# Gate's last and up's first pass, and the scores of two heads, as 64-row pairs on one TensorE array

## The chip, the core and the metric

The kernel runs on one core of a Trainium2 chip. The metric is the device time of one execution in microseconds (us). The core has five engines that run side by side and meet at semaphores: TensorE (PE in the profile, its weight loads PEld), VectorE (DVE), ScalarE (ACT), GpSimd (POOL) and SyncE (SP), which here issues all transfers.

## The reference, cut to what matters

The input is 2048 rows of width 576. Each row is normalised. One branch is causal attention with 32 heads of 18 columns and a window of 256; the other is a bilinear unit of inner width 4608. The output is the input plus their gated product.

```python
qkv = (xn @ wqkv).reshape(B, S, 3, 32, 18)...
scores = einsum("bhqd,bhkd->bhqk", q, k) * 18 ** -0.5      # kept where 0 <= i - j < 256
s = einsum("bhqk,bhkd->bhqd", softmax(scores), v)... @ wo
h = (xn @ w_gate) * (xn @ w_up)
out = x + s * silu(h @ w_down)
```

## The kernel before, in words

**Numbers in two parts.** A float32 operand is kept as two float16 parts, high and low, and a product is made of several float16 passes that add up in one PSUM bank. The normalised input, transposed, lies in `XT`: chunks 0 to 3 are the high parts of features 0 to 511, chunks 5 to 8 their low parts, and chunk 4 has the high parts of the last 64 features in rows 0 to 63 and their low parts in rows 64 to 127. A weight tile `upw` (128 output features) has ten chunks in the same manner: 0 to 4 high, 5 to 9 low; its chunks 4 and 9 hold the last 64 features twice, once in each half of the rows. `w_x_passes` (line 162) lists 14 passes of 128 rows: the 13 of `passes`, and at last chunk 9 of the weights with chunk 4 of `XT`, which adds low weight x high input and low weight x low input of the last 64 features.

**The prologue** (to about 220 us) normalises and transposes, and makes the values (`v_tile`) and queries and keys (`qk_tile`, nine groups `m` by four chunks `c` of 512 rows), which go to DRAM (`qk_d`, `v_d`).

**The main part** is a list of 72 slots: 18 groups `g` of 256 inner features by 4 chunks `c` of 512 rows. A slot has 16 places. The four weight tiles of a slot (gate, up, gate, up) take four places each; in every place the loop at line 716 issues a quarter of the 14 passes and then whatever `todo` has for that place, in the order in which `at(slot, place, f, ...)` put it there. Engines keep this order. Gate's sum is taken out by ScalarE (`gate_out`), up's by VectorE, which multiplies it with gate's (`up_out`). Both use the two PSUM banks named `up` in turn. `down` (line 593) multiplies the result with the down weights, in eight groups of six passes of 288 columns in the slot behind.

**The attention** is spread over slots 1 to 64 and a little beyond: step `s` takes two heads (`j`) and 512 queries, in four blocks `i` of 128 queries by up to 384 keys. `load_k`, `load_q` and `load_v` fetch a slot ahead through SP. `score` (line 486) makes one matmul with 72 contracted rows into one of two PSUM banks `s`, then VectorE masks and takes the largest (`sm`, `mx`, line 495). In the steps of the first chunk there are no earlier keys, so block 0 has 128 columns and block 1 has 256. Queries stand in the 72 rows as high, high, low, low and keys as high, low, high, low. `probs` (ScalarE), `turn_probs` (VectorE or GpSimd for the low part, then a transposing transfer `pt`) and `weigh` (six passes of 37 columns a block on TensorE) follow 2, 4 and 12 places behind the score; `finish` (VectorE and GpSimd) ends the step.

```python
        for n in range(8):
            j, i = divmod(n, 4)
            p = 2 * n
            at(b, p, score, s, j, i)
            at(b, p + 2, probs, s, j, i)
            at(b, p + 4, turn_probs, s, j, i)
            at(b, p + 12, weigh, s, j, i)
```

**The end** (from 1647 us) multiplies the attention with `wo` (`o_out`, line 680) and writes the output. At the very start, `keep_warm` (line 109) issues full passes on zeros, and between them two small float32 matmuls (lines 361 and 366) spread the largest value of the weights over the partitions; the second contracts a single row.

Of the kernel before, what the change touches and what calls it, by code (L numbers as in the profile page):

```python
# [11 lines left out]
F16 = mybir.dt.float16  # L12
# [8 lines left out]
def kernel(  # L21
# [10 lines left out]
    nc = tc.nc  # L32
    x = x[0]
    out = out[0]
    S, D = x.shape
# [29 lines left out]
    const = ctx.enter_context(tc.tile_pool(name="const", bufs=1))  # L65
# [7 lines left out]
    qk_d = [dram.tile([8, 2 * DH, S], F16, name=f"qk_d{i}") for i in range(H // 4)]  # L73
    v_d = dram.tile([S, H * VW], F16, name="v_d")
    o_d = [dram.tile([512, 2 * D], F16, name=f"o_d{i}") for i in range(NCH)]

    XT = const.tile([128, 9, S], F16, name="XT")
    ident = const.tile([128, 128], F32, name="ident")
    ones = const.tile([128, 128], F32, name="ones")

# [5 lines left out]
    def up_ring():  # L86
        return ring.tile([128, 10, 128], F16, name="upw", bufs=8)
# [10 lines left out]
    def bank(name, bufs, shape=(128, 512), dt=F32):  # L98
        return psum.tile(list(shape), dt, name=name, bufs=bufs)
# [43 lines left out]
    def hi(w, rv, s):  # L143
        nc.scalar.activation(w, rv, AF.Copy, scale=s)  # L144

    def lo(w, rv, s, h):
        nc.vector.scalar_tensor_tensor(w, rv, s, h, op0=OP.mult, op1=OP.subtract)  # L147
# [8 lines left out]
    def passes(a, b):  # L156
        r = [(a[:, k], b[:, k]) for k in range(5)]
        r += [(a[:, k], b[:, 5 + k]) for k in range(4)]
        r += [(a[:, 5 + k], b[:, k]) for k in range(4)]
        return r  # L160

    def w_x_passes(w, c):
        b = XT[:, :, c * 512:(c + 1) * 512]
        return passes(w, b) + [(w[:, 9], b[:, 4])]
# [56 lines left out]
    def turn(t):  # L221
        nc.sync.dma_start(XT[:, :, t * 128:(t + 1) * 128], XN.pop(t), transpose=True)

# [11 lines left out]
    def v_tile(t):  # L235
        pv = [bank(("s", "dn", "up", "pv")[t % 4], 2) for _ in range(2)]
        xt = XT[:, :, t * 128:(t + 1) * 128]
        ps = [(b, a) for a, b in passes(wv, xt)] + [(xt[:, 4], wv[:, 9])]
# [19 lines left out]
    UW, DW, RAW, HT, GT, SC = {}, {}, {}, {}, {}, {}  # L258

    def qk_split(m):  # L260
        if m < QM:
            w = UW["q", m] = up_ring()
            r = rqk[:, :, m * 128:(m + 1) * 128]
            hi(w[:, 0:5], r, ps_qk[:, 2:3])
            lo(w[:, 5:10], r, ps_qk[:, 2:3], w[:, 0:5])
# [3 lines left out]
    def qk_tile(w, m, c):  # L269
        ps = bank("up", 2)  # L270
        pl = w_x_passes(w, c)
        for i, (a, b) in enumerate(pl):
            nc.tensor.matmul(ps, a, b, start=i == 0, stop=i == len(pl) - 1)  # L273
        if c == 0:
            QP[m] = qpool.tile([128, 2, S], F16, name="qp", bufs=2)
        q = QP[m][:, :, c * 512:(c + 1) * 512]
        nc.scalar.activation(q[:, 0], ps, AF.Copy, scale=PROJ)  # L277
        nc.vector.scalar_tensor_tensor(q[:, 1], ps, PROJ, q[:, 0], op0=OP.mult, op1=OP.subtract)  # L278
# [20 lines left out]
    def ffn_amax(g, kind, half):  # L299
        if (g, "am") not in SC:  # L300
            SC[g, "am"] = ring.tile([128, 2, 3], F32, name="am", bufs=2)
        r = RAW[g, kind]
        r = r[:, half] if kind == 2 else r[:, :, half * 128:(half + 1) * 128]
        nc.vector.tensor_reduce(SC[g, "am"][:, half, kind:kind + 1], r, axis=AX.X if kind == 2 else AX.XY,  # L304
                                op=OP.max, apply_absolute_value=True)

    def ffn_spread_out(g):
        am = SC.pop((g, "am"))
        nc.vector.tensor_tensor(am[:, 0], am[:, 0], am[:, 1], op=OP.max)
        spread_out(f"f{g}", am[:, 0], 3)  # L310

    def ffn_spread_in(g):
        SC[g, "sp"] = spread_in(f"f{g}", ring, 3)
# [112 lines left out]
    for m in range(QM):  # L426
        for c in range(NCH):
            qk_tile(UW["q", m], m, c)
            if c == 1:
                qk_split(m + 2)  # L430
            if m == 1 and c < 3:
                ffn_amax(0, c, 0)
                ffn_amax(0, c, 1)
            if m == 2 and c == 0:
                ffn_spread_out(0)
            if m == 3 and c == 0:
                ffn_spread_in(0)
                ffn_scale(0)
            if m >= QM - 2 and c >= 2:
                k = 2 * (m - QM + 2) + c - 2  # L440
                up_hi(0, k)
                up_lo(0, k)
        qk_store(m)
        del UW["q", m]
# [3 lines left out]
    att = att_stack.enter_context(tc.tile_pool(name="att", bufs=1))  # L448
# [3 lines left out]
                            fill=-3e38, base=0, channel_multiplier=-1)  # L452
    nc.gpsimd.affine_select(bias[:, 256:384], bias[:, 256:384], pattern=[[-1, 128]], compare_op=OP.is_ge,
                            fill=-3e38, base=0, channel_multiplier=1)
    QS, KS, VT, SM, PP, PT, PVB, OB = {}, {}, {}, {}, {}, {}, {}, {}


    def load_k(s):
        c, u = s // 16, 2 * (s % 16) + H
        k0 = max(0, c * 512 - 256)  # L460
        n = (c + 1) * 512 - k0
        KS[s] = att.tile([128, 2, 768], F16, name="ks", bufs=2)
        d = KS[s][:, :, 768 - n:]
        for a in (0, 36):
            nc.sync.dma_start(d[a:a + 36],
                              qk_d[u // 8][u % 8:u % 8 + 2, :, k0:k0 + n].rearrange("j r n -> r j n"))

    def load_q(s):
        c, u = s // 16, 2 * (s % 16)
        d = QS[s] = att.tile([128, 2, 512], F16, name="qs", bufs=2)  # L470
        for a, r0, r1 in ((0, 0, 18), (18, 0, 36), (54, 18, 36)):
            nc.sync.dma_start(d[a:a + r1 - r0],
                              qk_d[u // 8][u % 8:u % 8 + 2, r0:r1, c * 512:(c + 1) * 512].rearrange("j r n -> r j n"))

    def load_v(s):
        c, p = s // 16, s % 16
# [6 lines left out]
    def first_kb(s):  # L483
        return 2 if s < 16 else 0

    def score(s, j, i):
        lo_ = max(first_kb(s), i) * 128
        hi_ = (i + 3) * 128
        n = hi_ - lo_
        ps = bank("s", 2)  # L490
        nc.tensor.matmul(ps[:, :n], QS[s][0:72, j, i * 128:(i + 1) * 128], KS[s][0:72, j, lo_:hi_],  # L491
                         start=True, stop=True)
        sm = att.tile([128, 384], F32, name="sm_", bufs=4)
        mx = att.tile([128, 2], F32, name="mx", bufs=3)
        nc.vector.tensor_tensor_reduce(sm[:, 384 - n:], ps[:, :n], bias[:, 384 - n:], 1.0, -3e38,  # L495
                                       op0=OP.add, op1=OP.max, accum_out=mx[:, 0:1])
        nc.gpsimd.tensor_scalar(mx[:, 1:2], mx[:, 0:1], sig[:, 1:2], shift, op0=OP.mult, op1=OP.add)  # L497
        SM[s, j, i] = (sm[:, 384 - n:], mx, n)
# [13 lines left out]
        nc.sync.dma_start(pt[:, 0:2 * n // 128], pp[:, 0:2 * n], transpose=True)  # L512

    def weigh(s, j, i):
        if j == 0 and i == 0:
            PVB[s] = bank("pv", 2, (128, 2, 4, 64))
        pt = PT.pop((s, j, i))
        lo_ = max(first_kb(s), i)
        nb = i + 3 - lo_
        for n in range(2 * nb):  # L520
            nc.tensor.matmul(PVB[s][:, j, i, :VW], pt[:, n], VT[s][:, lo_ + n % nb, j * VW:(j + 1) * VW],  # L521
                             start=n == 0, stop=n == 2 * nb - 1)
# [32 lines left out]
    def at(slot, place, f, *a):  # L555
        todo.setdefault(slot * 16 + place, []).append((f, a))

    first_slot = 1
    for s in range(NSTEP):
        b = first_slot + s  # L560
        at(b - 1, 1, load_k, s)
        at(b - 1, 3, load_q, s)
        at(b - 1, 13, load_v, s)
        for n in range(8):
            j, i = divmod(n, 4)
            p = 2 * n
            at(b, p, score, s, j, i)
            at(b, p + 2, probs, s, j, i)
            at(b, p + 4, turn_probs, s, j, i)
            at(b, p + 12, weigh, s, j, i)  # L570
        at(b, 31, finish, s)

    def gate_out(sl, ft, ps):
        g = f_ring("gt")
# [35 lines left out]
    for g in range(NG):  # L610
        b = 4 * g - 4
# [104 lines left out]
    for sl in range(NSLOT + 1):  # L716
        g, c = divmod(sl, NCH)
        for place in range(16):
            if sl < NSLOT:
                k, quarter = divmod(place, 4)  # L720
                if quarter == 0:
                    ps = bank("up", 2)
                    pl = w_x_passes(UW[g, k], c)
                n0 = (14 * quarter + 3) // 4
                n1 = (14 * (quarter + 1) + 3) // 4
                for i in range(n0, min(n1, 14)):
                    a, b = pl[i]
                    nc.tensor.matmul(ps, a, b, start=i == 0, stop=i == 13)  # L728
                if quarter == 3:
                    (gate_out if k % 2 == 0 else up_out)(sl, k // 2, ps)  # L730
                    if c == NCH - 1:
                        del UW[g, k]
            for f, a in todo.pop(sl * 16 + place, []):
                f(*a)
# [33 lines left out]
```

## Time and profile before

| what | before |
|---|---|
| time, median of 3 runs | 1719.51 us (1718.47 to 1720.28) |
| profiled execution: its own time | 1717.89 us |
| profiled execution: span from first to last instruction | 1716.0 us |
| granted TensorE clock, mean | 0.993 |
| TensorE matmuls | 12299 |
| VectorE, ScalarE, GpSimd busy | 73%, 53%, 24% |
| DMA, mean rate | 124 GB/s |

A page of the profile gives one execution: busy time of each engine, the span in slices, the chain of work that ended last, and the costliest groups of instructions. Matmuls are pipelined: one lasts longer than the distance to the next, so their busy times overlap and a price is read from the distance of starts. In the windows, a line has the stretch, then the sum of busy time, then the busy time and count for PE, PEld, DVE, ACT and POOL, the granted clock, the share of the DMA engines and GB/s. In the timeline, a line has start, duration, engine, line, operation, operands and count, and in brackets the idle time before it with what ended it.

### The profile page before, as it was taken

The page shows a single profiled execution, that of the slowest core. Times are in us where ns is not written, and L with a number is a line of the kernel's source. Part 1 is how long each engine was busy: PE and PEld are TensorE (multiplying, and loading weights), DVE is VectorE, ACT ScalarE, POOL GpSimd, SP SyncE. Part 2 cuts the span into 40 slices and gives each one's busy share as a digit, 9 for nine tenths or more (in the row PEclk, how much of TensorE's full clock was granted, in tenths as well). Part 3 has the DMA queues.
Part 4 walks back from the last instruction along what each step waited for, and adds up shares of the span by engine and source line. Part 5 has one row for each costly group of instructions (what it writes and reads, how often), then busy time and mean ns, then how long its engine had stood idle before and what let it go on. Part 6 is the DMA issues. An engine that isn't in the chain of part 4 may idle for free.

```text
span 1716.0 us, 34567 instructions
## 1 busy us (share of the span) xinstructions
PE 1682.3 (98%) x12299; PEld 993.8 (58%) x12299; DVE 1250.8 (73%) x3150; ACT 908.6 (53%) x1562; POOL 403.7 (24%) x870
## 2 busy tenths in 40 slices
PE   6999999999999999999999999999999999999999
PEld 3744445555555555555555555555555555555567
DVE  6442367777878888888878888888888878765544
ACT  4422346555565656565656565666666665632230
POOL 2200013322232323232323232322223222320000
PEclk8999999999999999999999999999999999999999
DMA  7942345464546665757586766657676767541228
GB/s 187 225 121 80 102 110 116 91 128 83 125 83 134 134 146 103 154 112 146 104 171 122 127 141 114 140 111 149 135 147 103 145 107 145 108 104 57 58 59 218
DMA packets 543109, 212.17 MB, mean 124 GB/s; under 512 B 479704, under 2 KB 523992, under 8 KB 542936
## 3 DMA queue, kind: packets, MB, share of 16 engines
q1 hardware_dynamic: 542936, 209.96, 58.2%
q8 instruction: 96, 1.57, 0.4%
q14 instruction: 77, 0.63, 0.1%
HBM read 82.30 MB, written 23.75 MB: 62 GB/s over the span
## 4 chain that ended last, share of the span: by engine, by line
PE 93%; DMA 3%; DVE 2%; SPq 1%; ACT 1%; issue 0%; POOL 0%; ACTq 0%; DVEq 0%
PE up L728 50%; PE dn L603 24%; PE up L273 6%; PE s L491 5%; PE pv L521 4%; PE dn L691 2%; PE up L691 1%; DMA sd_qk<-am_qk 1%; SPq L287 1%; DMA XT<-xh 0%; DMA raw<-in_B_w_gate_dram 0%; DMA xr<-in_A_x_dram 0%; PE s L241 0%; DMA spread<-sd_qk 0%; ACT xn L217 0%
## 5 line engine op out<-in xcount | busy, mean ns | idle before, releaser
L728 PE MATMUL up<-XT,upw 128*128 128x512 f16 x4032 | 1048.5, 379 | 2.4 <-DVE ht L580 2.4
L728 PEld LDWEIGHTS <-upw 128*128 128x128 f16 x4032 | 390.8, 97 | 283.8 <-issue 4.5
L603 PE MATMUL dn<-dnw,hh 128*128 128x288 f16 x3432 | 513.3, 286 | 0.8 <-DVE acc L608 0.8
L603 PEld LDWEIGHTS <-hh 128*128 128x128 f16 x3456 | 336.9, 97 | 192.8 <-issue 0.9
L608 DVE SCALAR_TENSOR_TENSOR acc<-dn,sc,acc 128x288 f32<-128x288 f32 x540 | 277.3, 514 | 165.1 <-PE dn L603 163.3
L497 POOL TENSOR_SCALAR mx<-mx,sig 128x1 f32<-128x1 f32 x512 | 179.7, 351 | 852.9 <-DVE mx L495 819.7
L521 PEld LDWEIGHTS <-pt 128*128 128x128 f16 x2880 | 147.5, 96 | 121.2 <-DMA pt<-pp 0.6
L491 PE MATMUL s<-ks,qs 72*128 72x384 f16 (+2 forms) x512 | 160.3, 313 | 1.3 <-DMA qs<-qk_d 1.3
L521 PE MATMUL pv<-vt,pt 128*128 128x37 f16 x2880 | 152.9, 179 | 0.2 <-DMA pt<-pp 0.2
L575 ACT ACTIVATE gt<-up 128x512 f32<-128x512 f32 x144 | 85.5, 594 | 102.5 <-PE up L728 102.4
L585 ACT ACTIVATE hh<-ht 128x512 f16<-128x512 f32 x144 | 89.7, 623 | 70.3 <-DVE ht L580 70.3
L273 PE MATMUL up<-XT,upw 128*128 128x512 f16 x504 | 110.8, 383 | 7.6 <-ACT upw L144 4.0
L580 DVE SCALAR_TENSOR_TENSOR ht<-up,gt 128x512 f32<-128x512 f32 x144 | 98.8, 686 | 12.9 <-PE up L728 12.4
L590 DVE SCALAR_TENSOR_TENSOR hh<-hh,ht 128x512 f16<-128x512 f16 x144 | 98.0, 681 | 0.0
L304 DVE TENSOR_REDUCE am<-raw 128x1 f32<-128x640 f32 (+1 forms) x108 | 85.3, 792 | 7.8 <-DMA raw<-in_B_w_gate_dram 5.4
L273 PEld LDWEIGHTS <-upw 128*128 128x128 f16 x504 | 49.7, 99 | 68.4 <-issue 7.2
L278 DVE SCALAR_TENSOR_TENSOR qp<-up,qp 128x512 f16<-128x512 f32 x36 | 24.9, 691 | 68.3 <-ACT qp L277 57.6
L277 ACT ACTIVATE qp<-up 128x512 f16<-128x512 f32 x36 | 21.5, 597 | 85.7 <-PE up L273 85.7
L147 DVE SCALAR_TENSOR_TENSOR upw<-raw,sc,upw 128x640 f16<-128x640 f32 x72 | 63.3, 880 | 0.1
L241 PEld LDWEIGHTS <-XT 128*128 128x128 f16 x448 | 45.1, 102 | 26.5 <-issue 8.3
L144 ACT ACTIVATE upw<-raw,sc 128x640 f16<-128x640 f32 x72 | 59.1, 824 | 0.0
L541 POOL CAST ob<-o 128x144 f16<-128x144 f32 x64 | 27.8, 435 | 102.4 <-DVE o L537 102.4
(2195 smaller groups left out, 1890.2 us busy)
## 6 DMA issues: line engine op xcount, KB each, us to landing
raw<-in_B_w_down_dram SPq DMA_DIRECT2D x18, 576.0 KB
ks<-qk_d SPq DMA_DIRECT2D x96, 108.0 KB
raw<-in_B_w_gate_dram SPq DMA_DIRECT2D x18, 512.0 KB
raw<-in_B_w_up_dram SPq DMA_DIRECT2D x18, 512.0 KB
pt<-pp SPq DMA_TRANSPOSE x512
qk_d<-qp SPq DMA_DIRECT2D x56, 144.0 KB
vt<-v_d SPq DMA_DIRECT2D x48, 111.0 KB
v_d<-vo SPq DMA_DIRECT2D x16, 296.0 KB
```

The source lines that it names most:

```text
L273: nc.tensor.matmul(ps, a, b, start=i == 0, stop=i == len(pl) - 1)
L304: nc.vector.tensor_reduce(SC[g, "am"][:, half, kind:kind + 1], r, axis=AX.X if kind == 2 else AX.XY, op=OP.max, apply_absolute_value=True)
L491: nc.tensor.matmul(ps[:, :n], QS[s][0:72, j, i * 128:(i + 1) * 128], KS[s][0:72, j, lo_:hi_], start=True, stop=True)
L497: nc.gpsimd.tensor_scalar(mx[:, 1:2], mx[:, 0:1], sig[:, 1:2], shift, op0=OP.mult, op1=OP.add)
L521: nc.tensor.matmul(PVB[s][:, j, i, :VW], pt[:, n], VT[s][:, lo_ + n % nb, j * VW:(j + 1) * VW], start=n == 0, stop=n == 2 * nb - 1)
L575: nc.scalar.activation(g, ps, AF.Copy, scale=G_SC)
L580: nc.vector.scalar_tensor_tensor(h, ps, U_SC, GT.pop((sl, ft)), op0=OP.mult, op1=OP.mult)
L585: nc.scalar.activation(hh[:, 0], h, AF.Copy, scale=1.0 / LO)
L590: nc.vector.scalar_tensor_tensor(hh[:, 1], hh[:, 0], -LO, h, op0=OP.mult, op1=OP.add)
L603: nc.tensor.matmul(ps[:, :HALF], a, b, start=q == 0, stop=q == len(l) - 1)
L608: nc.vector.scalar_tensor_tensor(d, ps[:, :HALF], SC[g][:, 9:10], d, op0=OP.mult, op1=OP.add)
L728: nc.tensor.matmul(ps, a, b, start=i == 0, stop=i == 13)
```

## The change

**Gate and up.** The 13 passes of `passes` stay as they are. The last pass of gate is cut to rows 0 to 63: chunk 9 of its weights by the high parts of the last 64 features. Up's own such pass becomes its first, on rows 64 to 127, with a copy of those high parts that lies in the new tile `XT2`. Both are issued one behind the other at the end of gate's four places, and the products of low by low parts are left out. The two banks of a gate and up pair are taken together at gate's start.

**Scores.** A head now has 54 rows: queries high, high, low by keys high, low, high. Head 0 of the step stands in rows 0 to 53, head 1 in rows 64 to 117. `score_pair` issues both heads' matmuls of a block at places 3, 7, 11 and 15; the VectorE work of head 0 follows there and that of head 1 two places later. The blocks go in the order block, head instead of head, block. Loads of keys and queries are eight a step instead of five. `load_v` and `finish` go one place back.

In the built program the matmuls and weight loads of the pairs address 64 x 128 parts of the array at rows 0 and 64, 400 of each; all other float16 matmuls address 128 x 128, as all did before.

```diff
+    XT2 = const.tile([128, S], F16, name="XT2")
...
+    def full_passes(w, c):
+        return passes(w, XT[:, :, c * 512:(c + 1) * 512])
+
+    def half_pass(w, c, upper):
+        r = slice(64, 128) if upper else slice(0, 64)
+        return w[r, 9], (XT2[r] if upper else XT[r, 4])[:, c * 512:(c + 1) * 512]
...
+            if m == 0:
+                nc.sync.dma_start(XT2[64:128, c * 512:(c + 1) * 512], XT[0:64, 4, c * 512:(c + 1) * 512])
...
     def load_k(s):
...
-        for a in (0, 36):
-            nc.sync.dma_start(d[a:a + 36],
-                              qk_d[u // 8][u % 8:u % 8 + 2, :, k0:k0 + n].rearrange("j r n -> r j n"))
+        for j in range(2):
+            for a, r1 in ((0, 36), (36, 18)):
+                nc.sync.dma_start(KS[s][64 * j + a:64 * j + a + r1, 768 - n:], qk_d[u // 8][u % 8 + j, 0:r1, k0:k0 + n])
 
     def load_q(s):
...
-        for a, r0, r1 in ((0, 0, 18), (18, 0, 36), (54, 18, 36)):
+        for j in range(2):
+            for a, r1 in ((0, 18), (18, 36)):
...
-        nc.tensor.matmul(ps[:, :n], QS[s][0:72, j, i * 128:(i + 1) * 128], KS[s][0:72, j, lo_:hi_],
-                         start=True, stop=True)
+    def score_pair(s, i):
+        lo_ = max(first_kb(s), i) * 128
+        hi_ = (i + 3) * 128
+        for j in range(2):
+            r = slice(64 * j, 64 * j + 54)
+            ps = SP[s, j, i] = bank("s", 2)
+            nc.tensor.matmul(ps[:, :hi_ - lo_], QS[s][r, i * 128:(i + 1) * 128], KS[s][r, lo_:hi_],
+                             start=True, stop=True)
...
-        at(b - 1, 13, load_v, s)
+        at(b - 1, 14, load_v, s)
         for n in range(8):
-            j, i = divmod(n, 4)
-            p = 2 * n
+            i, j = divmod(n, 2)
+            p = 2 * n + 3
+            if j == 0:
+                at(b, p, score_pair, s, i)
             at(b, p, score, s, j, i)
...
-        at(b, 31, finish, s)
+        at(b, 32, finish, s)
...
-                if quarter == 0:
-                    ps = bank("up", 2)
-                    pl = w_x_passes(UW[g, k], c)
-                n0 = (14 * quarter + 3) // 4
-                n1 = (14 * (quarter + 1) + 3) // 4
-                for i in range(n0, min(n1, 14)):
+                up, w = k % 2, UW[g, k]
+                if place % 8 == 0:
+                    banks = bank("up", 2), bank("up", 2)
+                pl = full_passes(w, c)
+                for i in range((13 * quarter + 3) // 4, (13 * (quarter + 1) + 3) // 4):
                     a, b = pl[i]
-                    nc.tensor.matmul(ps, a, b, start=i == 0, stop=i == 13)
+                    nc.tensor.matmul(banks[up], a, b, start=i == 0 and not up, stop=i == 12 and up == 1)
+                if quarter == 3 and not up:
+                    nc.tensor.matmul(banks[0], *half_pass(w, c, False), start=False, stop=True)
+                    nc.tensor.matmul(banks[1], *half_pass(UW[g, k + 1], c, True), start=True, stop=False)
                 if quarter == 3:
-                    (gate_out if k % 2 == 0 else up_out)(sl, k // 2, ps)
+                    (up_out if up else gate_out)(sl, k // 2, banks[up])
```

More of the change, by code (lines that the diff above doesn't have):

```diff
@@ L454 @@
                             fill=-3e38, base=0, channel_multiplier=1)
-    QS, KS, VT, SM, PP, PT, PVB, OB = {}, {}, {}, {}, {}, {}, {}, {}
+    QS, KS, VT, SP, SM, PP, PT, PVB, OB = {}, {}, {}, {}, {}, {}, {}, {}, {}
     def load_k(s):
@@ L461, in load_k @@
         n = (c + 1) * 512 - k0
-        KS[s] = att.tile([128, 2, 768], F16, name="ks", bufs=2)
-        d = KS[s][:, :, 768 - n:]
-        for a in (0, 36):
-            nc.sync.dma_start(d[a:a + 36],
-                              qk_d[u // 8][u % 8:u % 8 + 2, :, k0:k0 + n].rearrange("j r n -> r j n"))
+        KS[s] = att.tile([128, 768], F16, name="ks", bufs=2)
+        for j in range(2):
+            for a, r1 in ((0, 36), (36, 18)):
+                nc.sync.dma_start(KS[s][64 * j + a:64 * j + a + r1, 768 - n:], qk_d[u // 8][u % 8 + j, 0:r1, k0:k0 + n])
     def load_q(s):
         c, u = s // 16, 2 * (s % 16)
-        d = QS[s] = att.tile([128, 2, 512], F16, name="qs", bufs=2)
-        for a, r0, r1 in ((0, 0, 18), (18, 0, 36), (54, 18, 36)):
-            nc.sync.dma_start(d[a:a + r1 - r0],
-                              qk_d[u // 8][u % 8:u % 8 + 2, r0:r1, c * 512:(c + 1) * 512].rearrange("j r n -> r j n"))
+        QS[s] = att.tile([128, 512], F16, name="qs", bufs=2)
+        for j in range(2):
+            for a, r1 in ((0, 18), (18, 36)):
+                nc.sync.dma_start(QS[s][64 * j + a:64 * j + a + r1],
+                                  qk_d[u // 8][u % 8 + j, 0:r1, c * 512:(c + 1) * 512])
     def load_v(s):
@@ L484, in first_kb, with score @@
         return 2 if s < 16 else 0
-    def score(s, j, i):
+    def score_pair(s, i):
         lo_ = max(first_kb(s), i) * 128
         hi_ = (i + 3) * 128
-        n = hi_ - lo_
-        ps = bank("s", 2)
-        nc.tensor.matmul(ps[:, :n], QS[s][0:72, j, i * 128:(i + 1) * 128], KS[s][0:72, j, lo_:hi_],
-                         start=True, stop=True)
+        for j in range(2):
[3 more added lines that the diff above has]
+                             start=True, stop=True)
+    def score(s, j, i):
+        ps = SP.pop((s, j, i))
+        n = (i + 3 - max(first_kb(s), i)) * 128
         sm = att.tile([128, 384], F32, name="sm_", bufs=4)
@@ L514, in weigh @@
     def weigh(s, j, i):
-        if j == 0 and i == 0:
+        if (j, i) == (0, 0):
             PVB[s] = bank("pv", 2, (128, 2, 4, 64))
```

## The prediction

> **What bounds the kernel now.** I read the page's header and chain first.
>
> ```profile
> span 1716.0 us, 34567 instructions
> PE 1682.3 (98%) x12299; PEld 993.8 (58%) x12299; DVE 1250.8 (73%) x3150; ACT 908.6 (53%) x1562; POOL 403.7 (24%) x870
> ...
> PE 93%; DMA 3%; DVE 2%; SPq 1%; ACT 1%; issue 0%; POOL 0%; ACTq 0%; DVEq 0%
> ```
>
> The reader is to see that TensorE is busy for 98% and carries 93% of the chain that ended last. The windows of the main part ask whether it ever waits there.
>
> ```profile
> 300.00:600.00 300.00, 300.00 (x2253) 177.34 (x2251) 234.58 (x646) 177.54 (x324) 89.21 (x194) 1.00 0.54 111
> ...
> 1200.00:1520.00 320.00, 320.00 (x2500) 189.58 (x2499) 262.79 (x670) 199.96 (x336) 91.80 (x198) 1.00 0.68 130
> 1520.00:1647.00 127.00, 127.00 (x768) 72.29 (x766) 66.28 (x130) 26.12 (x42) 4.07 (x12) 1.00 0.21 48
> ```
>
> It doesn't: the busy time (the second number) equals the stretch. VectorE (the fourth) is at 78 to 82% until 1520 us. So time taken from or put on TensorE in the slots counts in full, until another engine is late. Busy times overlap, so a matmul's price is the distance to the next start.
>
> ```profile
> 1535.97 1.51 PE up L728 x7
> ...
> 799.46 0.10 PEld L491 LDWEIGHTS <-qs 72*128 72x128 f16 x1
> 799.48 0.32 PE L491 MATMUL s<-ks,qs 72*128 72x384 f16 x1
> 799.49 0.26 PEld L728 LDWEIGHTS <-upw 128*128 128x128 f16 x2
> 799.64 0.38 PE L728 MATMUL up<-XT,upw 128*128 128x512 f16 x1
> ```
>
> Seven 512-column passes stand for 1.51 us in the chain, 0.216 us each. A 384-column score is followed after 0.16 us, though it lasts 0.32. And the next weight load starts 0.01 us after a matmul has started: it lies under that matmul and costs nothing.
>
> **What is removed.** *Passes.* 18 weight groups x 4 chunks x 2 gate and up pairs make 144 pairs. Each gives up two full passes and gets two 64-row passes of 512 columns. If those run side by side, one pass is saved: 144 x 0.216 = 31.1 us.
>
> *Scores.* There are 512.
>
> ```profile
> L491 PE MATMUL s<-ks,qs x512: 216/322/497, 218.8 to 1519.9; 72*128 72x384 f16 x150, 72*128 72x128 f16 x11, 72*128 72x256 f16 x10
> ...
> L491 PE MATMUL s<-ks,qs 72*128 72x384 f16 (+2 forms) x512 | 160.3, 313 | 1.3 <-DMA qs<-qk_d 1.3
> ```
>
> By the code 32 have 128 columns, 32 have 256 and 448 have 384. At 0.16 us, and the short ones in proportion (0.05 and 0.11), they take 71.7 + 3.5 + 1.7 = 77 us. Pairing would save half: 38.5. Together 31.1 + 38.5 = 69.6 us over 144 + 256 = 400 pairs, 0.174 us a pair. Going from 72 to 54 rows by itself saves nothing: a pass lasts by its columns.
>
> **What is added on TensorE.** Each pair stands between full-array groups (behind a gate pass and before `weigh`, or behind `weigh` and before `down` or passes), so there are 800 changes between the full array and its halves. No trace row shows this change in float16. The nearest are the two small float32 matmuls at the start: line 366 contracts one row, between full-array warming passes of line 112.
>
> ```profile
> 12.04 0.28 DVE L363 TENSOR_REDUCE mrow<-up 1x1 f32<-1x128 f32 x1 [0.55 <-PE up L361]
> 12.22 0.63 PE L112 MATMUL pv<-idle 128*128 128x512 bf16 x1
> 12.78 0.28 PEld L366 LDWEIGHTS up<-mrow,ones 1*128 1x128 f32 x1 [0.84 <-DVE mrow L363]
> 13.02 0.35 PE L366 MATMUL up<-mrow,ones 1*128 1x1 f32 x1
> 13.30 0.10 PEld L112 LDWEIGHTS <-idle 128*128 128x128 bf16 x1
> ...
> 13.70 1.06 PE L112 MATMUL pv<-idle 128*128 128x512 bf16 x2
> ...
> 13.30:15.00 1.70, 1.70 (x5) 0.58 (x5) 1.46 (x6) 0.83 (x2) 0.00 (x0) 0.50 0.93 347
> ```
>
> *Going in.* The page puts L366's wait down to VectorE, but that had ended at 12.04 + 0.28 = 12.32. The load came at 12.78. Two full passes take 1.06 us and one 0.63, so one streams for 0.43; that of 12.22 streamed until 12.65. So a load for a part of the array did not slip under the matmul ahead: it came 0.13 us after its columns had gone in. *Coming out.* The second one-column matmul starts at 13.02, the full-array load at 13.30: 0.28 later instead of 0.01. Part of this may be the slow float32 load of the matmul itself (0.35 to 0.5 us for two), so it is an upper bound. The granted clock was 0.50 there (column after POOL's), against 1.00 in the slots; a pass streams in 0.43 there and 0.216 here. Taking the array's emptying to go with its clock, as the streaming does, I halve both: 0.065 in, 0.14 out. The bounds: nothing at all below, 0.13 + 0.28 unhalved above.
>
> The Trainium skill, "TensorEngine Tiling (Array Packing)", section Key Properties, says that a change of tiling mode drains TensorE. It gives no price; going in, the late load at 12.78 agrees with it.
>
> *The load that nothing hides.*
>
> ```profile
> 39.62 0.41 PE L241 MATMUL pv<-wv,XT 128*128 128x288 f16 x2
> ...
> 39.90 0.24 PEld L241 LDWEIGHTS <-XT 128*128 128x128 f16 x3 [0.19 <-DMA XT<-xh]
> 39.91 0.42 PE L241 MATMUL s<-wv,XT 128*128 128x288 f16 x2
> ```
>
> After a wait for a transfer the load stands open: the matmul starts 0.01 behind it and the first pair of passes takes 0.42 rather than 0.41. So an open load costs about 0.02 us. A pair has three: going in, the second half's behind the first's, and coming out: 0.06.
>
> *Sum.* A pair costs 0.065 + 0.14 + 0.06 = 0.265 us more than its columns, x 400 = 106 us. Less the 69.6 saved: 36 us slower. On the profiled execution's own time of 1717.9 (its span is 1716.0) this is 1754; the median of the runs shown is 1.6 higher, so I say 1755.5.
>
> **What is moved or added elsewhere costs nothing.** *VectorE and the score banks.* Both banks are now filled at place 4i + 3, but the second is read two places later and wanted back two places after that.
>
> ```profile
> 1009.93 0.32 PE L491 MATMUL s<-ks,qs 72*128 72x384 f16 x1
> ...
> 1011.79 0.54 DVE L495 CUSTOM_DVE_ANT_0 sm__13875<-s,bias 128x384 f32<-128x384 f32 x1
> ...
> 1012.50 0.32 PE L491 MATMUL s<-ks,qs 72*128 72x384 f16 x1
> ```
>
> This is one of the latest reads, behind the work of `finish` and a split of down weights: it ends at 1012.33, 2.4 us after its place, and two places are 2.57. So a cover of 0.17 us is left in such a step and more in others. Were VectorE later, both score matmuls would wait and TensorE's whole queue with them: each 0.3 us too late once a step is 64 x 0.3 = 19 us, which I take at nothing, since slower slots give VectorE more room. *Up's bank* is opened one pass earlier, when `up_out` has had most of four places to empty it. *SP.* A step issues eight loads of queries and keys instead of five.
>
> ```profile
> 806.86 0.90 SPq L465 DMA_DIRECT2D ks<-qk_d  x2
> ...
> 809.77 1.06 SPq L472 DMA_DIRECT2D qs<-qk_d  x3
> ...
> SPq L512 <- DVE pp L510: 282.9, 162, 3.1
> ```
>
> At 0.35 to 0.45 us each, three more are 1.3 us in a step of 16 places, 20.5 us. Behind them stand the transposes of the probabilities, which wait for VectorE's `pp` for 283 us in total, so the queue has room, and `weigh` comes eight places (10 us) after its transpose was asked for. The loads are a slot early, and 108 rows of each instead of 144 move. If the cover failed, 64 steps x 1.3 = 83 us would be the limit. The four copies into `XT2` are issued during the first projection, long before slot 0. `score`, `load_v` and `finish` move by up to three places with all that follows them, which only shifts the attention by 4 us inside slots that end 127 us before the last.
>
> **Rivals.** *1, faster: no drain.* The row-tiled load may slip ahead like any other, float32 having been the reason at 12.78. Then a pair costs at most its three open loads, 0.06 x 400 = 24 us, and the change gives 46: 1674. With these hidden too it gives 69.6: 1650. It decides for this side as soon as both changes of a pair together take less than 0.174 − 0.06 = 0.114 us. For it: TensorE's loads are early everywhere else, and the exit row is clouded by the float32 load. Against: VectorE's end at 12.32 explains nothing of the entry at 12.78. The Trainium skill, "TensorE: Matmul & The Clock Gate", Part 3, has row tiles start about 4 ns apart, with a measured 3.07 times for four; no run here shows it, and by it alone this rival's 1650 would hold.
>
> *2, much slower: the halves take turns.* If the second half streams after the first, nothing is saved and the 106 us stay: 1717.9 + 106 = 1824. For it: no two matmuls in this trace run side by side. Against: they share neither rows nor banks. The same time comes from a drain that does not go with the clock: 0.13 + 0.28 + 0.06 = 0.47, x 400 = 188, less 69.6: 1836.
>
> *3, no difference:* both ways cost 0.065, with 0.06 of loads 0.19 a pair: 76 − 69.6 = 6 slower, 1724; a little less and it is even.
>
> **How the numbers follow.** Forecast (a drain each way that goes with the clock, 1724 to 1790, the upper end with half of the unhalved excess): 0.60. Rival 1: 0.24. Rival 2 with the unhalved drain: 0.12. Rival 3, even: 0.04. About 0.2% is what a measurement of this kernel can tell from no change. So faster 0.24, same 0.04, slower 0.72. A range from 1674 to 1824 leaves out the lower half of rival 1 and a part of rival 2, together under 2 in 10; the forecast's own is 1724 to 1790.
>
> **What the profile after would show.** Right: the load of each half pair starts after the columns of the matmul ahead are through, not 0.01 us after its start, and the load of the full group behind it likewise; the two halves start within 0.03 us of each other; the windows stay full, as these gaps lie inside the modelled ends of matmuls, and a slot between 300 and 1500 us takes about 0.5 us more than before. Wrong: loads that stay early around pairs (rival 1), a second half that starts 0.2 us after the first (rival 2), TensorE waiting for VectorE's reads of the scores, or for keys and queries.

## The result, and the profile after

The changed kernel takes 1733.64 us (median of 4 runs, 1733.52 to 1733.91) against 1719.55 for the kernel before: 14.1 us slower, a ratio of 1.0083 with a 95% interval of 1.0065 to 1.0100. The forecast was 36 us slower; the direction was right, the size 2.5 times too large. The measured time lies in the lower part of the stated range of 1724 to 1790.

The page's header and chain of the changed kernel:

```profile
span 1732.1 us, 34687 instructions
...
PE 1695.7 (98%) x12299; PEld 961.2 (55%) x12299; DVE 1229.2 (71%) x3150; ACT 901.8 (52%) x1562; POOL 417.5 (24%) x870
...
PE 93%; DMA 3%; DVE 2%; SPq 1%; ACT 1%; issue 0%; POOL 0%; ACTq 0%; DVEq 0%
```

Still 98% busy and 93% of the chain: what changed is the length of TensorE's own work. In the windows of the main part the busy time still fills the stretch, though the gaps below are in it: they are hidden by the modelled ends of matmuls, and only distances of starts show them.

```profile
300.00:600.00 300.00, 300.00 (x2219) 168.88 (x2218) 226.93 (x640) 171.90 (x318) 89.77 (x192) 1.00 0.51 107
```

The counts tell more: 2219 matmuls stand in this stretch, 2253 stood in it before. A part of this is that the changed kernel comes to 300 us some 5 us earlier in its list of work, so slots are compared below.

One pair of gate and up in the timeline of the changed kernel (start, duration; L747 are full passes, L750 and L751 the halves, L539 the weighing passes behind):

```profile
559.91 0.38 PE L747 MATMUL up<-XT,upw 128*128 128x512 f16 x1
560.22 0.09 PEld L750 LDWEIGHTS <-upw 64*128 64x128 f16 x1 [0.42 <-issue]
560.23 0.09 PEld L751 LDWEIGHTS <-upw 64*128 64x128 f16 x1
560.23 0.39 PE L750 MATMUL up<-XT,upw 64*128 64x512 f16 x1
560.23 0.39 PE L751 MATMUL up<-XT,upw 64*128 64x512 f16 x1
...
560.54 0.10 PEld L539 LDWEIGHTS <-pt 128*128 128x128 f16 x1 [0.23 <-issue]
560.55 0.19 PE L539 MATMUL pv<-vt,pt 128*128 128x37 f16 x1
```

The full pass of 559.91 has streamed by 560.12 (0.213 us for 512 columns: the full pass behind a score pair starts 0.266 after its second half with 384 columns and 0.159 with 128, so 256 columns take 0.107); the load for the first half comes 0.1 later, at 560.22. Both halves start together. They have streamed at 560.44; the full-array load behind them comes at 560.54, 0.1 later again. Two loads that were under the matmul ahead now stand open. A score pair looks the same (L505, with the down passes L623 behind):

```profile
1009.65 0.34 PE L505 MATMUL s<-ks,qs 54*128 54x384 f16 x2
1009.92 0.30 PE L623 MATMUL dn<-dnw,hh 128*128 128x288 f16 x1
...
1030.30 0.34 PE L505 MATMUL s<-ks,qs 54*128 54x384 f16 x2
```

Two 384-column scores in 0.27 us, where each alone took 0.16: side by side, yet 0.1 behind. The same block one slot later starts at 1030.30: a slot with attention takes 20.65 us, against 20.50 before. In the slots without attention only the gate and up pairs are left. Here are the first full passes of two neighbouring slots there, of the changed kernel and then of the kernel before:

```profile
1610.06 0.38 PE L747 MATMUL up<-XT,upw 128*128 128x512 f16 x1
...
1628.02 0.38 PE L747 MATMUL up<-XT,upw 128*128 128x512 f16 x1
```

```profile
1594.19 0.38 PE L728 MATMUL up<-XT,upw 128*128 128x512 f16 x1
...
1612.16 0.38 PE L728 MATMUL up<-XT,upw 128*128 128x512 f16 x1
```

17.96 and 17.97: there the change does nothing. So the loss sits in the scores. From the starts of each slot: 0.307 us in each of the 15 slots after slot 1 that have the scores of the first chunk (these are shorter, so that pairing saves less), 0.146 in most others with attention, together some 11.4. Nearly all the rest of the 16.1 between the two profiled spans is the prologue (slot 0 starts 3.7 later, 1.6 of it before the change touches anything) and one wait at slot 1.

### The profile page after: what moved, and what is told of

The parts are those of the page before. It is cut to its first block, busy times and chain, and to the rows that moved or that the text cites. A ratio compares the mean times of both kernels' runs of the same rounds, so it can differ in the third digit from the quotient of the medians.

```text
span 1732.1 us, 34687 instructions
## 1 busy us (share of the span) xinstructions
PE 1695.7 (98%) x12299; PEld 961.2 (55%) x12299; DVE 1229.2 (71%) x3150; ACT 901.8 (52%) x1562; POOL 417.5 (24%) x870
## 4 chain that ended last, share of the span: by engine, by line
PE 93%; DMA 3%; DVE 2%; SPq 1%; ACT 1%; issue 0%; POOL 0%; ACTq 0%; DVEq 0%
PE up L747 46%; PE dn L623 26%; PE up L283 6%; PE pv L539 5%; PE s L505 4%; PE up L750 3%; PE dn L711 2%; PE up L711 1%; SPq L297 1%; DMA sd_qk<-am_qk 1%; DMA XT<-xh 0%; DMA xr<-in_A_x_dram 0%; PE s L251 0%; DMA spread<-sd_qk 0%; DMA raw<-in_B_w_gate_dram 0%
## 5 line engine op out<-in xcount | busy, mean ns | idle before, releaser
L747 PE MATMUL up<-XT,upw 128*128 128x512 f16 x3744 | 902.3, 379 | 0.0
L747 PEld LDWEIGHTS <-upw 128*128 128x128 f16 x3744 | 366.4, 98 | 337.5 <-issue 2.4
L623 PE MATMUL dn<-dnw,hh 128*128 128x288 f16 x3432 | 515.7, 286 | 0.8 <-DVE acc L628 0.8
L515 POOL TENSOR_SCALAR mx<-mx,sig 128x1 f32<-128x1 f32 x512 | 163.8, 320 | 843.6 <-DVE mx L513 755.5
L623 PEld LDWEIGHTS <-hh 128*128 128x128 f16 x3456 | 295.8, 97 | 113.1 <-issue 42.6
L539 PEld LDWEIGHTS <-pt 128*128 128x128 f16 x2880 | 137.1, 96 | 119.6 <-issue 28.3
L539 PE MATMUL pv<-vt,pt 128*128 128x37 f16 x2880 | 154.2, 180 | 0.0
L283 PE MATMUL up<-XT,upw 128*128 128x512 f16 x504 | 112.5, 387 | 8.6 <-ACT upw L146 4.6
L283 PEld LDWEIGHTS <-upw 128*128 128x128 f16 x504 | 50.1, 99 | 70.7 <-issue 9.9
L505 PE MATMUL s<-ks,qs 54*128 54x384 f16 (+2 forms) x512 | 83.6, 323 | 0.1
L751 PE MATMUL up<-XT,upw 64*128 64x512 f16 x144 | 55.6, 386 | 4.5 <-DVE ht L600 4.5
```

Source lines behind the costliest of these rows:

```text
L505: nc.tensor.matmul(ps[:, :hi_ - lo_], QS[s][r, i * 128:(i + 1) * 128], KS[s][r, lo_:hi_], start=True, stop=True)
L623: nc.tensor.matmul(ps[:, :HALF], a, b, start=q == 0, stop=q == len(l) - 1)
L747: nc.tensor.matmul(banks[up], a, b, start=i == 0 and not up, stop=i == 12 and up == 1)
```

## The experiments

The kernel before was run again beside the experiments, with a median of 1720.45 us beside the first four and of 1721.67 beside the last two; each ratio is to the kernel before that ran beside it, and differences to the changed kernel are differences of medians.

**Theory A**, formed from that trace: a change from the whole array to its halves and back costs a fixed price, whatever the pair does; the halves do run side by side. Medians of the distances of starts over all pairs: 0.312 from a full 512-column pass to the half pass, instead of 0.216 (in: 0.096); 0.003 between halves; 0.318 to 0.319 from the second half to the next full matmul (out: 0.105 over the 0.213 that stream); and the first full matmul after it is followed 0.012 later than its like. That is 0.216 a pair for gate and up, within 0.001 the pass saved; 0.206 for scores (0.110 to 0.111 instead of 0.025 behind a 37-column pass), more than the 0.162 or less that they save. **Theory B**: these changes of mode, between the whole array and its halves, are cheap, and the loss comes from the new order, the later reads by VectorE and the additional loads.

**Pairs of gate and up only**, scores as before:

```diff
-                    nc.tensor.matmul(ps, a, b, start=i == 0, stop=i == 13)
+                    nc.tensor.matmul(banks[up], a, b, start=i == 0 and not up, stop=i == 12 and up == 1)
+                if quarter == 3 and not up:
+                    nc.tensor.matmul(banks[0], *half_pass(w, c, False), start=False, stop=True)
+                    nc.tensor.matmul(banks[1], *half_pass(UW[g, k + 1], c, True), start=True, stop=False)
```

> Only the gate and up half passes run in pairs; scores as before (72 rows, whole array). Theory A (each change between the whole array and its halves costs a fixed price, read in the trace after as 0.096 in and 0.117 out for such a pair, 0.003 between the halves; nothing else matters): a pair pays 0.216 and saves 0.216, so 1719 to 1721 us, no difference from before, and a slot without attention takes 17.96 us as before. Theory B (the changes cost little, the loss comes from the new order of the scores, their later reads by VectorE and the eight loads): the pairs' gain shows here, up to 31 us, 1689. The recorded forecast's price of 0.265 a pair would give 1727.

Measured: 1721.06 us against 1720.45, a ratio of 1.0009 (0.9999 to 1.0018). As theory A has it: 31 us of passes are saved and paid back.

**Scores over all rows**, the changed kernel's order, loads and places kept:

```diff
-            nc.tensor.matmul(ps[:, :hi_ - lo_], QS[s][r, i * 128:(i + 1) * 128], KS[s][r, lo_:hi_],
+            nc.tensor.matmul(ps[:, :hi_ - lo_], QS[s][:, j, i * 128:(i + 1) * 128], KS[s][:, lo_:hi_],
```

> The changed kernel with its order, loads and places, but each head's score contracts all 128 rows of the array (queries padded with zero rows in a tile of their own, keys of both heads as loaded), so the scores change no mode. Theory A: a score pair costs 0.086 + 0.003 + 0.117 = 0.206 and saves 0.162 (384 columns), 0.108 (256) or 0.055 (128); without it a slot gets 0.155 us shorter, and 0.32 in the first sixteen: 48 x 0.155 + 16 x 0.32 = 12.5 us, 1721. Theory B: order and loads stay, so 1733.

Measured: 1720.10, a ratio to the kernel before of 0.9999 (0.9990 to 1.0009), so 13.5 less than the changed kernel. Order, loads and later reads cost nothing that the time shows: theory B falls. (From the second chunk of rows on, a slot even takes 20.47 us, 0.03 less than before.) This is also the answer on the cover that the prediction named for them.

**Score pair straight behind the half pair** at places 3 and 11:

```diff
+            if j == 0 and i % 2 == 0:
+                beside[b * 16 + p] = s, i
...
                     nc.tensor.matmul(banks[1], *half_pass(UW[g, k + 1], c, True), start=True, stop=False)
+                    if sl * 16 + place in beside:
+                        score_pair(*beside.pop(sl * 16 + place))
```

> The changed kernel, but at places 3 and 11 the score pair is issued straight behind the gate and up half pair, ahead of the weighing passes, so both share one way in and one way out. Theory A: 128 x (0.086 + 0.117) = 26 us less than the changed kernel, 1708, faster than before by 12. Theory B: 1733, as only 0.15 us of order changes. If the price is for every matmul on a half rather than for the change of mode: 1733 too.

Measured: 1710.06, ratio 0.9943 (0.9926 to 0.9959): 23.6 less than the changed kernel, and faster than before. One of these places in its timeline (L753 and L754 are the halves, L505 the scores):

```profile
554.33 0.38 PE L750 MATMUL up<-XT,upw 128*128 128x512 f16 x1
554.64 0.09 PEld L753 LDWEIGHTS <-upw 64*128 64x128 f16 x1 [0.42 <-issue]
...
554.65 0.39 PE L753 MATMUL up<-XT,upw 64*128 64x512 f16 x1
554.65 0.39 PE L754 MATMUL up<-XT,upw 64*128 64x512 f16 x1
554.66 0.10 PEld L505 LDWEIGHTS <-qs 54*128 54x128 f16 x2
554.87 0.33 PE L505 MATMUL s<-ks,qs 54*128 54x384 f16 x2
555.13 0.22 PEld L539 LDWEIGHTS <-pt 128*128 128x128 f16 x6 [0.37 <-issue]
```

Within the mode the score loads are early again, 0.01 us after the halves start, and the scores follow the halves at 0.22, one pass's length. One way in, one way out, for four matmuls. So the price belongs to the change of mode, not to a matmul on a half. A slot of the later chunks takes 20.24 us here against 20.65 in the changed kernel, and the 0.41 is two ways in and out, as theory A has it. The 2.3 or so that are missing from the 26 are lost once, at slot 1, which takes 25.8 us against 23.5: there TensorE waits 5.7 us for VectorE instead of 4.5, and the granted clock behind that wait is 0.54 from 230 to 234 us, where it is 0.78 in the changed kernel.

**The same, and the lone blocks over all rows** (places 7 and 15):

```diff
-            r = slice(64 * j, 64 * j + 54)
+            r = slice(64 * j, 64 * j + 54) if i % 2 == 0 else slice(0, 128)
```

> As the adjacent version, and the other two blocks of a step (places 7 and 15) have their scores over all 128 rows of the array, with zero-padded queries, so that no pair stands alone. Theory A: 112 lone pairs of 384 columns lose 0.044 each and 16 of 256 lose 0.1: 6 to 7 us less than the adjacent version, 1701 to 1702. Theory B: no less than the adjacent version.

Measured: 1703.39, ratio 0.9898 (0.9883 to 0.9913): 6.7 less again. This version is 17 us faster than the kernel before and 30 faster than the changed one.

**Halves apart**: gate and up pairs only, but each half alone at the end of its own four places.

```diff
+                if quarter == 3:
+                    nc.tensor.matmul(banks[up], *half_pass(w, c, up == 1), start=False, stop=True)
```

> As the version with gate and up pairs only, but each half pass is issued alone at the end of its own four places, so that nothing runs beside it and each pays its own way in and out. Theory A: a pair costs 0.096 + 0.213 + 0.003 + 0.117 - now two single halves at 0.096 + 0.213 + 0.117 = 0.43 each: 144 x 0.43 = 61 us more than the pairs-only version (1721), 1782. If two halves streamed one after the other even as a pair (the recorded rival 2): 144 x 0.21 = 31 us more, 1752. If only a pair pays, not a single half: no more than 31, too.

Measured: 1779.42 us, ratio 1.0342 (1.0299 to 1.0385): 58.4 more than with pairs, against 61 expected and 31 if the halves of a pair took turns. A single half pays what a pair pays:

```profile
465.12 0.09 PEld L739 LDWEIGHTS <-upw 64*128 64x128 f16 x1 [0.42 <-issue]
465.13 0.39 PE L739 MATMUL up<-XT,upw 64*128 64x512 f16 x1
465.44 0.24 PEld L613 LDWEIGHTS <-hh 128*128 128x128 f16 x3 [0.23 <-issue]
```

**One-row probes** price the row from which the prediction took its emptying times:

```diff
+    def one_row(src):
+        ps = bank("pv", 2)
+        nc.tensor.matmul(ps[:, 0:1], src[0:1, 0:128], src[0:1, 0:1], start=True, stop=True)
...
+            if m == 5 and i == 6 and c in (1, 2):
+                one_row(idle if c == 1 else ones)
```

> The kernel before with three added matmuls that contract one row, between full passes: one in bfloat16 among the warming passes at half the clock (behind line 366's), one in bfloat16 and one in float32 in the queries' and keys' projection at the full clock. It prices the step of the prediction that halved the row of line 366. If emptying goes with the clock and float32 has no part in it: 0.13 and 0.28 at the half clock in bfloat16 as well, 0.065 and 0.14 at the full. If the way out was float32's own load (theory A reads about 0.1 out at the full clock after a pair): bfloat16 out is far under 0.28 at the half clock, and float32 stays longer than bfloat16 at the full clock. If the emptying does not go with the clock: the same figures at both clocks. The time stays within 3 us of before.

The time was 1720.88 us in one run. Its timeline, bfloat16 at the half clock, then bfloat16 and float32 at the full clock (L117 the probes; L112 and L277 the passes around), with the windows that give the granted clock (column after POOL's):

```profile
13.82 0.63 PE L112 MATMUL pv<-idle 128*128 128x512 bf16 x1
14.38 0.10 PEld L117 LDWEIGHTS <-idle 1*128 1x128 bf16 x1 [0.84 <-issue]
14.49 0.10 PEld L112 LDWEIGHTS <-idle 128*128 128x128 bf16 x1
...
163.56 0.59 PE L277 MATMUL up<-XT,upw 128*128 128x512 f16 x2
164.09 0.09 PEld L117 LDWEIGHTS <-idle 1*128 1x128 bf16 x1 [0.42 <-issue]
164.19 0.10 PEld L277 LDWEIGHTS <-upw 128*128 128x128 f16 x1
...
167.01 0.38 PE L277 MATMUL up<-XT,upw 128*128 128x512 f16 x1
167.32 0.29 PEld L117 LDWEIGHTS pv<-ones 1*128 1x128 f32 x2 [0.42 <-issue]
167.63 0.11 PEld L277 LDWEIGHTS <-upw 128*128 128x128 f16 x2
```

```profile
13.40:15.00 1.60, 1.60 (x6) 0.46 (x6) 1.34 (x6) 0.71 (x2) 0.00 (x0) 0.50 0.93 351
163.40:165.00 1.60, 1.60 (x9) 0.65 (x8) 0.61 (x1) 0.00 (x0) 0.00 (x0) 1.00 0.52 161
```

*Way in.* At the half clock the pass of 13.82 streams until 14.25, and the load comes at 14.38: 0.13. At the full clock the second pass starts at 163.78 (163.56 + 0.59 less the 0.38 that one lasts), streams until 163.99, and the load comes at 164.09: 0.10. Float32 at the full clock: 167.01 + 0.21 = 167.22, load at 167.32: 0.10. *Way out* in bfloat16: 14.38 to 14.49 at the half clock, 164.09 to 164.19 at the full: 0.11 and 0.10. The probe's own load fills 0.10 and 0.09 of that, so these are upper bounds. Float32 takes 0.31 from its first load to the full-array load, and its own two loads fill 0.29 of that. The same holds for line 366 in the kernel before: its two loads end at 13.28, and the full-array load came at 13.30.

```profile
12.78 0.50 PEld L366 LDWEIGHTS up<-mrow,ones 1*128 1x128 f32 x2 [0.84 <-DVE mrow L363]
```

The changed kernel has one score pair at the half clock, behind its wait at slot 1, where the way out can be read without such a load:

```profile
228.40:229.10 0.70, 0.70 (x3) 0.29 (x4) 0.53 (x4) 0.68 (x3) 0.00 (x0) 0.50 0.03 9
...
228.52 0.26 PE L505 MATMUL s<-ks,qs 54*128 54x128 f16 x1
...
228.70 0.13 PEld L747 LDWEIGHTS <-upw 128*128 128x128 f16 x2
```

The second half's 128 columns stream in 0.11 at this clock (a quarter of a pass's 0.43), until 228.63, and the full-array load comes 0.08 later, against 0.10 behind all pairs at the full clock. So emptying the array goes with the clock only in small part on the way in, and takes no longer at the half clock on the way out; and the 0.28 of line 366 was float32's load.

## Why the prediction was right or wrong

*Right: what is removed.* The halves start 0.003 us apart in the median (560.23 and 560.23 above) and stream together. The saving of 69.6 us was there: by distances of starts it is 144 x 0.216 + 39 = 70.

*Right: that the array empties, both ways.* The load at 12.78 was read rightly against the page's own attribution to VectorE: the probe's entry shows the same delay with no VectorE wait near. The Trainium skill, "TensorEngine Tiling (Array Packing)", Key Properties, says a change of tiling mode drains TensorE: all pairs here agree, with 0.1 us each way as its price. Rival 1 (no drain) is out. The figure of the Trainium skill, "TensorE: Matmul & The Clock Gate", Part 3, of about 4 ns between the starts of row tiles, agrees with the 3 ns here.

*Wrong: the price of a pair*, 0.265 predicted, 0.216 (gate and up) and 0.206 (scores) measured:

| term of the sum, us a pair | predicted | measured |
|---|---|---|
| emptying, in | 0.065 | 0.09 (scores 0.08) |
| emptying, out | 0.14 | 0.10 |
| three open loads | 0.06 | 0.02 |

The step that failed most is "the load that nothing hides". I priced it at 0.02 for each of three: the 0.01 from load to matmul plus the 0.01 by which the passes behind were longer, both rounded up from rows of two decimals (0.004 and 0.011 in the trace of the kernel before). In the pairs the first half follows its load by 0.004, the second half follows the first by 0.003 since its load runs beside the first half's, and coming out it is 0.004 + 0.012. That is 0.04 x 400 = 15 us too much. The emptying was wrong twice, by halving with the clock (in: too little; there is hardly any dependence) and by taking float32's load for emptying (out: too much); the two nearly cancel, and leave 0.01 to 0.02 x 400 = 5 us or so too much. The measured terms give 144 x 0.216 + 256 x 0.206 = 84 us, less 70: 14 slower. That this meets the 14.1 so closely is partly luck: the slots with attention hold 11.4 us of it (13.3 against the scores over all rows, whose slots are shorter than before), and what slot 1 and the prologue add is in no term of the sum. A slot grew by 0.15 to 0.31 us, where the prediction named about 0.5.

Rival 3, with 0.19 a pair, was nearer to the measured 0.21 than the forecast, by two errors that nearly cancel: it took both ways at 0.065 and the loads at 0.06. The upper end of the range, 1790, is by its own words 1754 + 41 = 1795; nothing hangs on it here.

*The point of decision.* The prediction had a pair break even at 0.174 us in the mean. It should have been read for the two kinds apart: gate and up pairs save 0.216 and pay 0.216, scores save 0.162 at most and pay 0.206. One kind was neutral, the other lost, and this is where the first two experiments part them.

*Right: the covers.* VectorE's later reads, the eight loads and the moved places cost nothing (scores over all rows: 0.9999). One exception, once: at slot 1 up's half pass, now one pass earlier in TensorE's queue, waits for VectorE.

```profile
226.50 0.82 DVE L314 TENSOR_REDUCE am<-raw 128x1 f32<-128x640 f32 x1 [3.42 <-DMA raw<-in_B_w_up_dram]
227.23 0.68 DVE L600 SCALAR_TENSOR_TENSOR ht<-up,gt 128x512 f32<-128x512 f32 x1
...
227.97 0.37 PE L751 MATMUL up<-XT,upw 64*128 64x512 f16 x1 [4.54 <-DVE ht L600]
```

VectorE stands behind a load of raw weights, and its `up_out` behind that. The kernel before had two waits at the same place, 2.4 us for VectorE (the page's group of L728) and 1.3 for queries (its group of L491), so slot 1 grew by 0.8. Rival 2 (the halves take turns) is out by the halves-apart run.

The 3.7 us by which slot 0 began later in the profiled execution of the changed kernel need no copies into `XT2` to come about. 2.1 of them lie in the projection of queries and keys, where the copies are issued; but the kernel of the one-row probes, which has no `XT2`, begins slot 0 at 208.4 us, against 208.1 in the changed kernel and 204.4 in the kernel before. Its two probes on the way take some 0.6. The same stretch of the projection, in the kernel before, the changed kernel and the one with probes:

```profile
143.00:146.40 3.40, 3.40 (x18) 1.53 (x16) 0.69 (x1) 0.60 (x1) 0.00 (x0) 1.00 0.07 10
143.00:146.40 3.40, 3.40 (x9) 1.22 (x9) 1.26 (x2) 0.00 (x0) 0.00 (x0) 0.50 0.00 0
143.00:146.40 3.40, 3.40 (x10) 1.22 (x8) 1.01 (x2) 0.00 (x0) 0.00 (x0) 0.50 0.00 0
```

Behind a wait of about 4 us that all three have, the granted clock was 0.50 here in two of them and 1.00 in the profiled execution of the kernel before. What decides this, and how often it happens, stays open.

## What to carry to other kernels

Pairs of matmuls on the two halves of the array save half of their columns' time, but here paid about 0.2 us to get the array into halves and back, so that a lone pair of 512 columns between full-array work was worth nothing, and a shorter one lost. Put all half-array work of a stretch in one block, so that one way in and out serves it (here 23.6 us), and leave what can't be put there on the whole array (here another 6.7). To price such a change, find the load that comes late, not the busy time: the gaps lie under the modelled ends of matmuls, and a slot's period or the distance of starts shows them where the busy time does not.

## What the runs showed of the hardware that was not expected

Emptying the array took 0.13 us on the way in at a granted clock of 0.50 and 0.10 at 1.00, and 0.08 at 0.50 and 0.10 at 1.00 on the way out, though a pass streams twice as fast at the full clock: most of it does not go with that clock. At 0.50 each of these is read from a single place. Within the mode of halves, loads for the same rows slip under running matmuls as on the whole array (554.66, 0.01 after the halves' start).
